# Exponential slots of two and two PSUM banks, and 576 instead of 456 score tiles on VectorE, in a kernel that mixes softmax attention with linear attention

## The chip, the cores and the metric

The kernel runs on one core of a Trainium2 chip, as one launch. The metric is device time in microseconds (us), the median of three runs. The engines of the core work side by side, each through its own list of instructions in a fixed order, and wait for each other by semaphores: TensorE (PE, with its weight loads as PEld) multiplies matrices into PSUM, ScalarE (ACT) computes exponentials, VectorE (DVE) and GpSimd (POOL) do elementwise work, and SP issues DMAs. PSUM has eight banks of 512 fp32 columns.

## What is computed

Two attention layers read the same input, and a gate per row mixes them. Layer B is softmax attention over 2048 rows with 32 heads of 16 columns; layer A is linear attention with a learned feature map.

```
def _B_ref(x, wqkv, wo):
    ...
    scores = jnp.einsum("bhqd,bhkd->bhqk", q, k) * (Dh ** -0.5)
    p = _softmax(scores, axis=-1)
    o = jnp.einsum("bhqk,bhkd->bhqd", p, v)
    return (lambda x, *d: x.transpose(*d))(o, 0, 2, 1, 3).reshape(B, S, D) @ wo
x = A_x
g = _sigmoid((x * gate_w).sum(-1, keepdims=True))
a = _A_ref(x, A_wqkv, A_w_phi, A_wo)
b = _B_ref(x, B_wqkv, B_wo)
return g * a + (1 - g) * b
```

In `_A_ref`, queries and keys go through a 16 by 16 matrix per head and two softmaxes over 16 features, and the sums over all rows are small matrices per head. Nearly all of the time goes into the scores of layer B: 32 heads of 2048 by 2048.

## The kernel before

**Tiles and blocks.** The scores are computed transposed, 128 keys by 512 queries at a time; such a score tile fills one PSUM bank. A block is four heads (one per 32-row strip of TensorE, `i`) with 512 queries; each of its heads has 16 tiles, so a block has 64 tiles, and there are 32 blocks, 2048 tiles. A score matmul (`qk_mm`, L782) uses 32 of the 128 rows, so that up to four of different heads run at once. A product matmul (`pv_mm`, L883) multiplies the exponentials with the values, 32 output columns per head, so that again four heads run at once; all products of a block add up in the one bank psO. A column of ones in the values gives the softmax's denominator.

**Two ways to an exponential.** Most tiles go through ScalarE. They are packed into slots (`slots`, filled by `next_tile`): an even slot has three tiles in the banks S0 to S2 of psS, an odd one has two in S3 and S4. `add_qk` (L786) writes a slot's scores, `add_exp` (L859, instruction at L862) takes them all in one instruction into the ring `Ebuf`, and `add_pv` (L903) multiplies the tiles of `PV_SETS` slots. Slot j+2 uses the banks of slot j. The other tiles go to VectorE, `DN[b]` of them in block b. `add_group` (L827) takes four at a time: for each, a matmul "dq" writes a score tile into a shared bank, and VectorE turns it into 16-bit integers whose bits, read as bf16, approximate the exponential (L840). Then two passes over the whole group (L853) add the constants STEPS, which gives two more such approximations. All three are multiplied with the values, three product matmuls ("terms") per tile instead of one.

**Shared banks.** psM and S5 (list `MISC`) are shared by the dq tiles and by every projection (`fill`, L591), such as keys, queries and values of layer B, the features of layer A (whose exponentials, L1105, run on ScalarE) and the output. psO is copied out at the end of a block (`add_norm`, L967), and only then may the next block's products begin.

**The order of the work.** It isn't written by hand. `Plan.add` notes for each operation an engine, an assumed duration, a priority and what it depends on. `Plan.layout` (L149) plays the program through with these durations and fixes each engine's order and each shared bank; `Plan.emit` writes the instructions and waits. In it, a dq tile may ride along with a round of scores if its strip is free and a bank is (`RIDE_TOL`); a scores operation has precedence when an exponential is due to end (`QK_TOL`, for even and odd slots); zero matmuls (`zero_mm`, L873) fill TensorE where its recent activity is low; and the VectorE passes of L853 and the products on GpSimd are kept apart (`lock`). A list of start points (`gates` and the constants ending in _AT and _PACE) ties projections to the exponential after which they may begin. Intermediate buffers are rings: four or so for the first result of a group and two or three for each of the other two (`rings`).

Of the kernel before, what the change touches and what calls it, by code (L numbers as in the profile page):

```python
# [27 lines left out]
STEPS = (35, 83)  # L28
ESCALE = math.log(2.0) / 2.0 ** 7

DN = (0, 10, 14, 16, 14, 16, 14, 16, 14, 16, 14, 16, 14, 16, 14, 16, 14, 16, 14, 16, 14, 16, 14, 16, 14, 16, 14, 16, 14, 16, 14, 12)
G_EARLY = 13
W_AT = 18.0
D_FIRST = 12
RIDE = 0.02
WINDOW = 3.41
ROWS = (0.0, 0.42, 0.65, 1.0, 1.15)
# [2 lines left out]
PE_CLASS = {"qk": 0, "dq": 0, "pv": 1, "term": 1, "zero": 1}  # L40
T_PRIO = 40.0
WARM = 4
DQ_PRIO, DQ_K = 0.0, 1.0
KG_AT, KG_PACE, QG_AT, QG_PACE = 40.0, 13.0, 270.0, 14.0
R1_AT, R1_PACE, R2_AT, R2_PACE, R3_AT, R3_PACE = 25.0, 14.0, 180.0, 14.0, 330.0, 25.0
TR_LAT, TR_ISSUE = 3.0, 0.4
OP_AT = 620.0
O_AT, O_PACE = 500.0, 10.0
PV_SETS = 3
RIDE_TOL = 0.22  # L50
DMA_PAD, T2_PAD = 1.0, 1.5
QK_TOL = (0.2, 0.65)
TURN_PAD = 4.0
G_DEEP = 6
K_AT, K_PACE, Q_AT, Q_PACE = 45.0, 13.0, 275.0, 13.5
PN = (1, 2, 1, 2, 1, 2, 1, 2, 1, 2, 1, 2, 1, 2, 1, 2, 1, 2, 1, 2, 1, 2, 1, 2, 1, 2, 1, 2, 1, 2, 1, 2)
D_AHEAD = 22.0
CONT = -60.0
EPAIRS = 5
ERING = 2 * EPAIRS  # L60
LAT, BANK_LAT = 0.12, 0.12
DVE_SCALE = 1.0
# [339 lines left out]
def _build(ctx, nc, A_x, A_wqkv, A_w_phi, A_wo, B_wqkv, B_wo, gate_w, out):  # L402
# [6 lines left out]
    def sem(name):  # L409
        return ctx.enter_context(nc.semaphore(name))  # L410

    xT = sb([128, KT, S], name="xT")
    WAT = sb([128, 8, D], name="WAT")
    Wp = sb([128, KT, 2 * D], name="Wp")
# [9 lines left out]
    vAf = sb([128, NT * 8 * 65], name="vA")  # L424
    vA = vAf[:].rearrange("p (a b c) -> p a b c", a=NT, b=8)
    phiK = sb([128, 8, 1024], name="phiK")
    Ebuf = sb([128, EPAIRS, 2560], name="E")
    Tx = sb([128, 2, 2048], name="Tx")
    EA = sb([128, 2, 1024], name="EA")
    half = sb([128, 64, 8], F32, name="half")  # L430
# [34 lines left out]
    bS = [Bank(f"S{i}", psS[:, 512 * i:512 * (i + 1)]) for i in range(6)]  # L465
    bO = Bank("O", psO[:])
    bM = Bank("M", psM[:])
    for b in range(3):
        bS[b].free = False
    FIRST = [bM, bO, bS[3], bS[4], bS[5]]  # L470
    EARLY = [bM, bO, bS[5]]
    MISC = [bM, bS[5]]

    P = Plan()

# [249 lines left out]

    while True:
        j = len(slots)
        act = [t for t in (next_tile() for _ in range(3 - j % 2)) if t is not None]
        if not act:
            break  # L730
        slots.append(act)
# [53 lines left out]

    def add_qk(j):  # L786
        ts = slots[j]
        base = 3 * (j % 2)
        reads = []
        for b, i, kt in ts:  # L790
            for k in (kkey(b // 8, kt), ("q", b // 2 % 4, b % 2)):
                if k not in reads:
                    reads.append(k)

        def fn(e):
            ins = None
            for m, t in enumerate(ts):
                ins = qk_mm(e, t, psS[:, 512 * (base + m):512 * (base + m + 1)])
            return ins
        op = P.add("pe", 0.25, -100, fn, reads=reads, writes=[("S", j % 2)], name=f"qk{j}")  # L800
        op.full = 0.21
        op.kind, op.heads = "qk", [t[1] for t in ts]
        if j < 2:
            op.margin = 0.1
        if j == 1:
            op.take = [bS[3], bS[4]]
        if j == 35:
            op.deps += xe
        return op

# [11 lines left out]

    def d_prio(d):
        b = d["t"][0]
        return first_slot[b] + d["k"] * 20.0 / DN[b] - D_AHEAD

    def add_group(g):  # L827
        t, s, m = (bufs[g[k]][0] for k in "tsm")
# [29 lines left out]

    def add_exp(j):  # L859
        n = len(slots[j])  # L860
        base = 3 * (j % 2)
        op = P.add("act", 0.051 + 0.4267 * n, 0.0, lambda e: e.activation(  # L862
            Ebuf[:, j // 2 % EPAIRS, 1536 * (j % 2):1536 * (j % 2) + 512 * n], psS[:, 512 * base:512 * (base + n)], ACTF.Exp, scale=ESCALE),
            reads=[("S", j % 2)], writes=[("E", j % ERING)], name=f"exp{j}")
        op.kind, op.extra = "exp", j % 2
        exp_ops[j] = op
        return op
# [35 lines left out]
    def add_pv(js):  # L903
        parts = {}
        for j in js:
            for m, t in enumerate(slots[j]):
                parts.setdefault(t[0], []).append((j, m, t))
        for b, jmts in parts.items():
            work, reads, seen = [], ["v1", "v2", "zero"], [0] * 4
            last = last_act[b] in [t for _, _, t in jmts]  # L910
            for j, m, t in jmts:
                start = (b, t[1]) not in pv_started
                pv_started.add((b, t[1]))
                o = 1536 * (j % 2) + 512 * m
                work.append((seen[t[1]], t, Ebuf[:, j // 2 % EPAIRS, o:o + 512], start))
                seen[t[1]] += 1
                for k in (("E", j % ERING), ("v", t[0] // 8, t[2] // 4)):
                    if k not in reads:
                        reads.append(k)
            rounds = max(seen)  # L920
            work.sort(key=lambda x: x[0])
            heads = [t[1] for n, t, _, _ in work if n == rounds - 1]
            cols = tuple(sum(x[0] == n for x in work) for n in range(rounds))
            work = [x[1:] for x in work]
            mts = [(m, t) for _, m, t in jmts]
            j = js[-1]

            opened_all = all((b, i) in pv_started for i in range(4))
            old = b in full_start

            def fn(e, work=work, last=last, j=j, b=b, old=old):
                ins = None
                for _ in range(zero_ops[j, b].extra):
                    zero_mm(e)
                for n, (t, rhs, start) in enumerate(work):
                    ins = pv_mm(e, t, rhs, start, last and n >= len(work) - 4)
                return ins
            first = any(t[1] == 0 and t[2] == 0 for _, t in mts)
            op = P.add("pe", 0.25 + 0.215 * (rounds - 1), -50, fn, reads=reads,
                       writes=["psO"] if first else (),  # L940
                       after=pv_last[-1:] + (block_pvd.get(b, []) if last else []), name=f"pv{j}")
            op.full = 0.215 * rounds
            op.kind, op.heads, op.cols = "pv", heads, cols
            op.room, op.alive = 2 if old else 0, opened_all and not last
            zero_ops[j, b] = op
            pv_last.append(op)
            if b not in full_start and all((b, i) in pv_started for i in range(4)):
                full_start[b] = op
                block_pvd[b] = []
                mine = [d for d in dtiles if d["t"][0] == b]  # L950
                for d in mine:
                    make_groups(d["g"]["n"] + 1)
                    assert made[0] > d["g"]["n"]
                    block_pvd[b] += add_pvd(d, op)
                if mine:
                    make_groups(mine[-1]["g"]["n"] + G_DEEP)
            if js[0] == 0:
                op.take = [bO]
            if first:
                op.margin = 1.0  # L960
            if last:
                add_norm(b, op)
# [82 lines left out]
    def out_last(i):  # L1045
# [9 lines left out]
                  writes=[("fin", tile % 4)], after=va_ops, name=f"Oe{tile}")  # L1055
        else:
            end = lambda e, ap: e.matmul(ap, lhsT=oT[:, 3, 3, 128 * i:128 * (i + 1)], rhs=WoB[:, 3, :], start=True, stop=True)
            f, mm = fill(-200 + i - 1.5, [end], [("oT", 3, 3), "WoB"], banks=bS[:5], name=f"O{tile}")
            drain(f, mm, "dve", 0.72, 0, lambda e, ap: e.scalar_tensor_tensor(
                fin[:, tile % 4, :], ap, omg[:, tile:tile + 1], osum[:, i - 2, :], ALU.mult, ALU.add),  # L1060
                  reads=["omg", ("part", i)], writes=[("fin", tile % 4)], after=va_ops, name=f"Oe{tile}")
# [167 lines left out]
        v_fill(0, c, 6.4 * c - 4.0, EARLY)  # L1229
    gates = {}  # L1230
    for qc in range(1, QC):
        gates[f"Q0.{qc}"] = 20 * qc
        q_fill(0, qc, 20.0 * qc)
    for c in range(QC):
        gates[f"K1.{c}"], gates[f"V1.{c}"] = int(R1_AT + R1_PACE * c), int(R1_AT + R1_PACE * (c + 4))
        k_fill(1, c, R1_AT + R1_PACE * c + 5)
        v_fill(1, c, R1_AT + R1_PACE * (c + 4) + 5)
        both = [v_pair(c, hf, R2_AT + R2_PACE * (c + 4 + hf / 2) + 5) for hf in range(2)]
        for hf in range(2):
            gates[f"V2.{c}.{hf}"] = int(R2_AT + R2_PACE * (c + 4 + hf / 2))  # L1240
        P.join_writes(both, ("v", 2, c))
        P.join_writes(both, ("v", 3, c))

    def k_row(r):
        at, pace = (R2_AT, R2_PACE) if r == 2 else (R3_AT, R3_PACE)
        for c in range(QC):
            gates[f"K{r}.{c}"] = int(at + pace * c)
            k_fill(r, c, at + pace * c + 5)

    gate()  # L1250
# [38 lines left out]
            k_row(k_next)  # L1289
            k_next += 1  # L1290
    for j in (NS - 2, NS - 1):
        exp_ops[j].rel = [bS[3 * (j % 2) + m] for m in range(3 - j % 2)]
    for op in P.ops:
        if op.name.startswith("Tq0."):
            op.deps = op.deps + wp_ops
# [7 lines left out]
    for op in P.ops:  # L1303
        if op.name.endswith(".0") and op.name[:-2] in gates:
            op.deps = op.deps + [exp_ops[gates[op.name[:-2]]]]
        for head, at, pace in (("P1.", KG_AT, KG_PACE), ("VA", KG_AT, KG_PACE), ("P0.", QG_AT, QG_PACE)):
            part = op.name[len(head):].split(".")
            if op.name.startswith(head) and len(part) == 2 and part[1] == "0" and part[0].isdigit():
                op.deps = op.deps + [exp_ops[min(NS - 40, int(at + pace * int(part[0])))]]

    P.idle, P.misc = zero_mm, MISC
    P.add("sp", 0.1, 1e6, lambda e: None, reads=[("out", i) for i in range(NT)], name="end")
# [36 lines left out]
```

## Time and profile before

| | |
|---|---|
| median of 3 runs | 777.43 us (777.22 to 778.01) |
| profiled execution, first to last instruction | 774.6 us |
| its mean granted TensorE clock | 0.991 |
| exponentials of 3 banks, of 2 banks | 318, 319 |
| conversions on VectorE (L840) | 456 |
| DMA | 30.72 MB, mean 40 GB/s |

The time of the profiled execution as a whole is not listed; its span lies 2.8 us below the median of the runs.

The page's second part cuts the span into 40 slices of 19.4 us, each digit the busy share in tenths:

```profile
PE   8999989998999999989999999998999998999999
...
DVE  3667877777778888567898897987887778787842
ACT  6999999999999999999999999999999999999996
...
PEclk9999999999999999998999999999999999999999
```

ScalarE is at 9 from the second slice to the last but one. VectorE is mostly at 7 or 8, with little to do in the first slice and the last two. TensorE's digits say less, because a matmul's row also holds the time in which it drains while the next one is already running. The trace gives the clock stretch by stretch: it is full except for three stretches at half speed, which begin about 345, 584 and 676 us from the start and last 6.8, 3.4 and 3.4 us.

Where a row is shown as "x318 | 518.2, 1629", 318 instructions were busy for 518.2 us and lasted 1629 ns each on average; rows of one engine can overlap at their ends, so the distance from start to start is what counts.

### The profile page before, as it was taken

The page shows a single profiled execution, that of the slowest core. Times are in us where ns is not written, and L with a number is a line of the kernel's source. Part 1 is how long each engine was busy: PE and PEld are TensorE (multiplying, and loading weights), DVE is VectorE, ACT ScalarE, POOL GpSimd, SP SyncE. Part 2 cuts the span into 40 slices and gives each one's busy share as a digit, 9 for nine tenths or more (in the row PEclk, how much of TensorE's full clock was granted, in tenths as well). Part 3 has the DMA queues.
Part 4 walks back from the last instruction along what each step waited for, and adds up shares of the span by engine and source line. Part 5 has one row for each costly group of instructions (what it writes and reads, how often), then busy time and mean ns, then how long its engine had stood idle before and what let it go on. Part 6 is the DMA issues. An engine that isn't in the chain of part 4 may idle for free.

```text
span 774.6 us, 17058 instructions
## 1 busy us (share of the span) xinstructions
PE 718.3 (93%) x7135; PEld 223.1 (29%) x7194; DVE 585.0 (76%) x1023; ACT 757.2 (98%) x708; POOL 137.0 (18%) x141
## 2 busy tenths in 40 slices
PE   8999989998999999989999999998999998999999
PEld 4332222332322222332322222222232222222222
DVE  3667877777778888567898897987887778787842
ACT  6999999999999999999999999999999999999996
POOL 6001032112322131200313121231311200000000
PEclk9999999999999999998999999999999999999999
DMA  6600000000000100201002221322311221020101
GB/s 128 146 9 16 20 14 21 10 23 9 10 17 9 24 8 8 72 8 23 23 27 60 55 71 44 82 68 51 83 53 38 73 53 37 22 64 3 46 13 48
DMA packets 67933, 30.72 MB, mean 40 GB/s; under 512 B 53208, under 2 KB 62808, under 8 KB 67856
## 3 DMA queue, kind: packets, MB, share of 16 engines
q1 hardware_dynamic: 66368, 28.95, 14.9%
q8 instruction: 56, 0.92, 0.5%
q10 hardware_dynamic: 1104, 0.66, 0.3%
q0 software_dynamic: 384, 0.02, 0.1%
q14 instruction: 21, 0.17, 0.1%
HBM read 7.87 MB, written 8.88 MB: 22 GB/s over the span
## 4 chain that ended last, share of the span: by engine, by line
ACT 84%; PE 11%; DVE 4%; SPq 1%; DMA 1%; issue 1%
ACT E_t L862 80%; ACT EA_t L1105 3%; PE psS L782 3%; PE psO L883 3%; PE psM L591 1%; PE psS L591 1%; DVE Tx_t L840 1%; DVE WAT_t L840 1%; PE psO L873 1%; DMA xT_t<-in_A_x_dram 1%; SPq L486 0%; DVE vA_t L853 0%; PE psS L651 0%; DVE vA_t L840 0%; DVE Ty_t L853 0%
## 5 line engine op out<-in xcount | busy, mean ns | idle before, releaser
L862 ACT ACTIVATE E_t<-psS 128x1536 bf16<-128x1536 f32 x637 | 731.9, 1419 | 5.4 <-PE psS L782 3.7
L782 PE MATMUL psS<-qz_t,kTB_t 32*128 32x512 bf16 x1815 | 277.0, 387 | 41.9 <-ACT E_t L862 34.1
L782 PEld LDWEIGHTS psS<-qz_t,kTB_t 32*128 32x128 bf16 x1815 | 69.2, 91 | 277.8 <-ACT E_t L862 242.3
L883 PE MATMUL psO<-E_t,vaug_t 128*32 128x512 bf16 (+1 forms) x1592 | 141.1, 389 | 0.7 <-DVE vaug_t L647 0.5
L840 DVE TENSOR_SCALAR Tx_t<-psS 128x512 int16<-128x512 f32 x121 | 82.4, 681 | 27.2 <-PE psS L782 24.6
L840 DVE TENSOR_SCALAR Tx_t<-psM 128x512 int16<-128x512 f32 x127 | 86.8, 683 | 19.4 <-PE psM L782 17.7
L873 PE MATMUL psO<-xT_t,zero_t 128*32 128x512 bf16 x1076 | 93.8, 387 | 0.0
L1110 POOL TENSOR_TENSOR half_t<-EA_t 128x512 f32<-128x512 bf16 x32 | 37.0, 1155 | 314.0 <-ACT EA_t L1105 273.4
L782 PE MATMUL psM<-qz_t,kTB_t 32*128 32x512 bf16 x233 | 90.1, 387 | 0.7 <-DVE Tx_t L840 0.2
L883 PE MATMUL psO<-vA_t,vaug_t 128*32 128x512 bf16 (+1 forms) x430 | 58.7, 387 | 0.0
L883 PE MATMUL psO<-Ty_t,vaug_t 128*32 128x512 bf16 (+1 forms) x308 | 50.4, 390 | 0.0
L1118 POOL TENSOR_TENSOR phiQ_t<-EA_t,stat_t 128x512 bf16<-128x512 bf16 x32 | 34.2, 1070 | 72.2 <-DVE stat_t L1114 61.7
L983 POOL TENSOR_TENSOR oT_t<-Tf_t,Rb_t 128x512 bf16<-128x512 f32 x15 | 19.1, 1272 | 157.4 <-DVE Ty_t L853 91.1
L883 PEld LDWEIGHTS psO<-E_t,vaug_t 128*32 128x32 bf16 (+1 forms) x1592 | 29.0, 95 | 59.8 <-issue 57.1
L1118 POOL TENSOR_TENSOR phiK_t<-EA_t,stat_t 128x512 bf16<-128x512 bf16 x32 | 33.8, 1058 | 60.4 <-DVE stat_t L1114 31.3
L883 PE MATMUL psO<-Tx_t,vaug_t 128*32 128x512 bf16 (+1 forms) x248 | 38.5, 398 | 0.0
L873 PEld LDWEIGHTS psO<-xT_t,zero_t 128*32 128x32 bf16 x1076 | 23.3, 94 | 41.3 <-issue 36.2
L853 DVE TENSOR_SCALAR vA_t<-Tx_t 128x2048 int16<-128x2048 int16 x50 | 34.1, 686 | 0.1
L853 DVE TENSOR_SCALAR Ty_t<-Tx_t 128x2048 int16<-128x2048 int16 x42 | 29.8, 709 | 0.4
L840 DVE TENSOR_SCALAR WAT_t<-psM 128x512 int16<-128x512 f32 x37 | 25.2, 682 | 5.9 <-PE psM L782 3.8
L840 DVE TENSOR_SCALAR WAT_t<-psS 128x512 int16<-128x512 f32 x39 | 26.6, 682 | 2.2 <-PE psS L782 1.9
L782 PEld LDWEIGHTS psM<-qz_t,kTB_t 32*128 32x128 bf16 x233 | 21.1, 91 | 23.1 <-issue 6.7
(188 smaller groups left out, 768.1 us busy)
## 6 DMA issues: line engine op xcount, KB each, us to landing
dpq<-phiQ_t SPq DMA_DIRECT2D x16, 256.0 KB, 2.1
Rb_t<-lr SPq DMA_DIRECT2D x120, 32.0 KB, 1.8
dpo<-oA_t SPq DMA_DIRECT2D x16, 128.0 KB, 1.8
qz_t<-qz_t SPq DMA_DIRECT2D x120, 16.0 KB, 1.8
Tf_t<-Tf_t SPq DMA_DIRECT2D x60, 32.0 KB, 2.0
out_dram<-WvA_t SPq DMA_DIRECT2D x14, 128.0 KB, 1.7
WB_t<-in_B_wqkv_dram SPq DMA_DIRECT2D x3, 384.0 KB, 4.4
WvA_t<-in_A_wqkv_dram SPq DMA_DIRECT2D x1, 512.0 KB, 4.0
```

Source lines behind the costliest of these rows:

```text
L591: return [lambda e, ap, i=i: e.matmul(ap, lhsT=lhs[i], rhs=rhs[i], start=(i == 0), stop=(i == len(lhs) - 1)) for i in range(len(lhs))]
L782: return e.matmul(bank, lhsT=kT_B[32 * i:32 * i + 32, b // 8 % 2, 128 * kt:128 * (kt + 1)], rhs=qz[32 * i:32 * i + 32, b // 2 % 4, b % 2, ...
L840: ops.append(drain(f, mm, "dve", 0.70, d_prio(d), lambda e, ap, q=q: e.tensor_scalar(quarter(tb, q).bitcast(I16), ap, EXPB, 0.0, op0=ALU.a ...
L853: add(0.72 if size == 4 else 0.45, lambda e, dst=dst, step=step: e.tensor_single_scalar(dst, t, step, ALU.add), tk, [g[key]], "D2" if key ...
L862: op = P.add("act", 0.051 + 0.4267 * n, 0.0, lambda e: e.activation(Ebuf[:, j // 2 % EPAIRS, 1536 * (j % 2):1536 * (j % 2) + 512 * n], psS ...
L873: ins = e.matmul((psO if bank is None else bank)[32 * i:32 * i + 32, :], lhsT=zero[:], rhs=xT[:, 0, 0:NQ], start=bank is not None, stop=ba ...
L883: return e.matmul(psO[32 * i:32 * i + w, :], lhsT=vaug[:, kt, o:o + w], rhs=rhs, start=start, stop=stop, tile_position=(0, 32 * i), skip_g ...
L983: P.add("pool", 1.1, -40, lambda e: e.tensor_tensor(oT[:, r, qc, :], Tf[:, 0, :], Rb[:], ALU.mult), reads=[("Tf", 0), "Rb"], writes=[("oT" ...
L1105: ins = e.activation(EA[:, b, :].rearrange("p (g s c) -> p s g c", s=2, c=64)[:, sgn, :, :], ap.rearrange("p (g c) -> p g c", c=64), ACTF. ...
L1110: P.add("pool", 1.15, prio, lambda e: e.tensor_tensor(half[:], e3[:, :, 0:8], e3[:, :, 8:16], ALU.add), reads=[("EA", b)], writes=["half"] ...
L1118: parts.append(P.add("pool", 1.0, prio, lambda e, n=n: e.tensor_tensor(dst[:, 512 * n:512 * n + 512].rearrange("p (g f) -> p g f", f=DH), ...
```

## The change

- The slots have two banks each: S0 and S1 for even ones, S2 and S3 for odd ones (`SIZES`). The ring `Ebuf` has six pairs of 2 + 2 tiles instead of five of 3 + 2.
- S4 becomes a shared bank: `MISC` is psM, S4 and S5.
- `DN` rises from 14 and 16 tiles in most blocks to 18 and 20 (22 and 20 in blocks 29 and 30), 576 in all instead of 456. Blocks 0, 1 and 31 keep 0, 10 and 12.
- Products are taken for four slots at a time (`PV_SETS`), which is eight tiles.
- What counts in slots is scaled by `SC` = 1.25: the gates, and the due times of the VectorE tiles.
- Some constants of the order change: `QK_TOL`, `DQ_K`, `G_EARLY` (the block from which another set of buffers is used), `G_DEEP` (how many groups may be entered ahead), `D_FIRST`, and the _AT and _PACE values.

No operation is added or dropped otherwise.

```diff
-DN = (0, 10, 14, 16, 14, 16, 14, 16, 14, 16, 14, 16, 14, 16, 14, 16, 14, 16, 14, 16, 14, 16, 14, 16, 14, 16, 14, 16, 14, 16, 14, 12)
-G_EARLY = 13
+DN = (0, 10, 18, 20, 18, 20, 18, 20, 18, 20, 18, 20, 18, 20, 18, 20, 18, 20, 18, 20, 18, 20, 18, 20, 18, 20, 18, 20, 18, 22, 20, 12)
+G_EARLY = 14
+SIZES = (2, 2)
+SC = 1.25
-D_FIRST = 12
+D_FIRST = 14
-DQ_PRIO, DQ_K = 0.0, 1.0
-KG_AT, KG_PACE, QG_AT, QG_PACE = 40.0, 13.0, 270.0, 14.0
+DQ_PRIO, DQ_K = 0.027, 1.299
-R1_AT, R1_PACE, R2_AT, R2_PACE, R3_AT, R3_PACE = 25.0, 14.0, 180.0, 14.0, 330.0, 25.0
+KG_AT, KG_PACE, QG_AT, QG_PACE = 41.939, 13.0, 270.429, 11.441
+R1_AT, R1_PACE, R2_AT, R2_PACE, R3_AT, R3_PACE = 36.575, 14.388, 170.604, 16.017, 313.139, 23.051
-OP_AT = 620.0
-O_AT, O_PACE = 500.0, 10.0
-PV_SETS = 3
+OP_AT = 641.751
+O_AT, O_PACE = 627.355, 10.348
+PV_SETS = 4
-QK_TOL = (0.2, 0.65)
+QK_TOL = (0.25, 0.2)
-G_DEEP = 6
-K_AT, K_PACE, Q_AT, Q_PACE = 45.0, 13.0, 275.0, 13.5
+G_DEEP = 8
+K_AT, K_PACE, Q_AT, Q_PACE = 41.797, 12.153, 275.0, 10.409
-EPAIRS = 5
+EPAIRS = 6
...
-    Ebuf = sb([128, EPAIRS, 2560], name="E")
+    Ebuf = sb([128, EPAIRS, 512 * (SZ[0] + SZ[1])], name="E")
...
-    FIRST = [bM, bO, bS[3], bS[4], bS[5]]
-    EARLY = [bM, bO, bS[5]]
-    MISC = [bM, bS[5]]
+    lowS = SIZES[0] + SIZES[1]
+    FIRST = [bM, bO] + bS[SIZES[0]:]
+    EARLY = [bM, bO] + bS[lowS:]
+    MISC = [bM] + bS[lowS:]
...
-        act = [t for t in (next_tile() for _ in range(3 - j % 2)) if t is not None]
+        act = [t for t in (next_tile() for _ in range(SZ[j % 2])) if t is not None]
...
-        base = 3 * (j % 2)
+        base = SZ[0] * (j % 2)
...
-        return first_slot[b] + d["k"] * 20.0 / DN[b] - D_AHEAD
+        return first_slot[b] / SC + d["k"] * 20.0 / DN[b] - D_AHEAD
...
-        gates[f"Q0.{qc}"] = 20 * qc
+        gates[f"Q0.{qc}"] = int(SC * 20 * qc)
```

The other lines replace 3 and 1536, as the size of an even slot, in the same manner, and scale the other gates by SC.

More of the change, by code (lines that the diff above doesn't have):

```diff
@@ L410, in sem @@
         return ctx.enter_context(nc.semaphore(name))
+    SZ = SIZES
     xT = sb([128, KT, S], name="xT")
@@ L467, in _build @@
     bM = Bank("M", psM[:])
-    for b in range(3):
+    for b in range(SIZES[0]):
         bS[b].free = False
-    FIRST = [bM, bO, bS[3], bS[4], bS[5]]
-    EARLY = [bM, bO, bS[5]]
-    MISC = [bM, bS[5]]
+    lowS = SIZES[0] + SIZES[1]
+    FIRST = [bM, bO] + bS[SIZES[0]:]
+    EARLY = [bM, bO] + bS[lowS:]
+    MISC = [bM] + bS[lowS:]
     P = Plan()
@@ L805, in add_qk @@
         if j == 1:
-            op.take = [bS[3], bS[4]]
-        if j == 35:
+            op.take = [bS[m] for m in range(SIZES[0], lowS)]
+        if j == int(35 * SC):
             op.deps += xe
@@ L860, in add_exp @@
         n = len(slots[j])
-        base = 3 * (j % 2)
+        base = SZ[0] * (j % 2)
         op = P.add("act", 0.051 + 0.4267 * n, 0.0, lambda e: e.activation(
-            Ebuf[:, j // 2 % EPAIRS, 1536 * (j % 2):1536 * (j % 2) + 512 * n], psS[:, 512 * base:512 * (base + n)], ACTF.Exp, scale=ESCALE),
+            Ebuf[:, j // 2 % EPAIRS, 512 * SZ[0] * (j % 2):512 * SZ[0] * (j % 2) + 512 * n], psS[:, 512 * base:512 * (base + n)], ACTF.Exp, scale=ESCALE),
             reads=[("S", j % 2)], writes=[("E", j % ERING)], name=f"exp{j}")
@@ L913, in add_pv @@
                 pv_started.add((b, t[1]))
-                o = 1536 * (j % 2) + 512 * m
+                o = 512 * SZ[0] * (j % 2) + 512 * m
                 work.append((seen[t[1]], t, Ebuf[:, j // 2 % EPAIRS, o:o + 512], start))
@@ L1057, in out_last @@
             end = lambda e, ap: e.matmul(ap, lhsT=oT[:, 3, 3, 128 * i:128 * (i + 1)], rhs=WoB[:, 3, :], start=True, stop=True)
-            f, mm = fill(-200 + i - 1.5, [end], [("oT", 3, 3), "WoB"], banks=bS[:5], name=f"O{tile}")
+            f, mm = fill(-200 + i - 1.5, [end], [("oT", 3, 3), "WoB"], banks=bS[:lowS], name=f"O{tile}")
             drain(f, mm, "dve", 0.72, 0, lambda e, ap: e.scalar_tensor_tensor(
@@ L1231, in _build @@
     for qc in range(1, QC):
-        gates[f"Q0.{qc}"] = 20 * qc
+        gates[f"Q0.{qc}"] = int(SC * 20 * qc)
         q_fill(0, qc, 20.0 * qc)
     for c in range(QC):
-        gates[f"K1.{c}"], gates[f"V1.{c}"] = int(R1_AT + R1_PACE * c), int(R1_AT + R1_PACE * (c + 4))
+        gates[f"K1.{c}"], gates[f"V1.{c}"] = int(SC * (R1_AT + R1_PACE * c)), int(SC * (R1_AT + R1_PACE * (c + 4)))
         k_fill(1, c, R1_AT + R1_PACE * c + 5)
@@ L1239, in _build @@
         for hf in range(2):
-            gates[f"V2.{c}.{hf}"] = int(R2_AT + R2_PACE * (c + 4 + hf / 2))
+            gates[f"V2.{c}.{hf}"] = int(SC * (R2_AT + R2_PACE * (c + 4 + hf / 2)))
         P.join_writes(both, ("v", 2, c))
@@ L1246, in k_row @@
         for c in range(QC):
-            gates[f"K{r}.{c}"] = int(at + pace * c)
+            gates[f"K{r}.{c}"] = int(SC * (at + pace * c))
             k_fill(r, c, at + pace * c + 5)
@@ L1291, in _build @@
     for j in (NS - 2, NS - 1):
-        exp_ops[j].rel = [bS[3 * (j % 2) + m] for m in range(3 - j % 2)]
+        exp_ops[j].rel = [bS[SZ[0] * (j % 2) + m] for m in range(SZ[j % 2])]
     for op in P.ops:
@@ L1308, in _build @@
             if op.name.startswith(head) and len(part) == 2 and part[1] == "0" and part[0].isdigit():
-                op.deps = op.deps + [exp_ops[min(NS - 40, int(at + pace * int(part[0])))]]
+                op.deps = op.deps + [exp_ops[min(NS - 40, int(SC * (at + pace * int(part[0]))))]]
     P.idle, P.misc = zero_mm, MISC
```

## The prediction

> **What bounds the kernel now.** I read the page's busy table first, then the chain that ended last, then the waits, then the groups by shape, then single rows in order of time.
>
> ```profile
> PE 718.3 (93%) x7135; PEld 223.1 (29%) x7194; DVE 585.0 (76%) x1023; ACT 757.2 (98%) x708; POOL 137.0 (18%) x141
> ...
> ACT 84%; PE 11%; DVE 4%; SPq 1%; DMA 1%; issue 1%
> ```
>
> ScalarE (ACT) has work in 757.2 of 774.6 us, and 84% of the chain lies on it. The waits (total us, times, longest us) show that almost nothing holds it up:
>
> ```profile
> ACT E_t L862 <- PE psS L782: 3.7, 5, 1.7
> ```
>
> So the sum starts from ScalarE's own rows. The two shapes of its exponential:
>
> ```profile
> L862 ACT ACTIVATE E_t<-psS 128x1536 bf16<-128x1536 f32 x318 | 518.2, 1629 | 4.9 <-PE psS L782 3.3 <-PE psM L782 1.4
> L862 ACT ACTIVATE E_t<-psS 128x1024 bf16<-128x1024 f32 x319 | 385.8, 1210 | 0.5 <-PE psS L782 0.4
> ```
>
> The means of 1629 and 1210 ns overlap with the next row and must not be added up. From start to start, where the next one follows without delay, a three-bank exponential takes 1.337 us and a two-bank one 0.909 us; the chain shows the same as single pieces:
>
> ```profile
> 157.55 1.34 ACT E_t L862
> ...
> 480.60 0.92 ACT E_t L862
> ```
>
> The span is 774.6 us and the median of the runs 777.43; I carry the 2.8 us between them along unchanged.
>
> **1. ScalarE gains 46.1 us.** 318 x 3 + 319 x 2 = 1592 score tiles are on ScalarE now, and 2048 - 1592 = 456 on VectorE. Then it is 576, which leaves 1472 tiles in 736 exponentials of two banks. Now: 318 x 1.337 + 319 x 0.909 = 715.1 us. Then: 736 x 0.909 = 669.0. The other ScalarE work is untouched. Alone this gives 777.4 - 46.1 = 731.3 us.
>
> The shorter form costs a little: 0.909 for two banks is 0.4545 per tile, 1.337 for three is 0.446, and the difference between the two forms, 0.428 per bank, leaves 0.053 us fixed per instruction. 99 more instructions cost 5 us, already in the sum. The Trainium skill, "ScalarE: Activation LUTs", section "What ACT_TABLE_LOAD costs", speaks more strongly against the change: 186 ns + 0.833 ns per column, less about 93 ns of overlap back to back, an estimate of 1.373 and 0.946 us, by which the gain would be 42.1 us instead of 46.1. The rows of this trace have less fixed cost, and the sum uses them.
>
> **2. The refill of a slot: 0 to 8 us.** A slot is refilled with scores while the other slot's exponential runs. So far the three-bank slot had 0.909 us for it and the two-bank slot 1.337. After a two-bank exponential, the next one started more than 0.97 us later 38 times out of 319. Without the last (before the end) and three beside half-speed stretches of the clock, that is 34 times and 6.3 us over the normal step. Then every refill has only 0.909 us: 736/319 x 6.3 = 14.5, or 8 us more. The lower end is nothing, since only two heads instead of three must be finished. This delay is no addition if another engine is later anyway.
>
> **3. VectorE gets 108.7 us.** A tile there costs one conversion out of PSUM (L840), and a group of four costs two further passes (L853).
>
> ```profile
> L840 DVE TENSOR_SCALAR Tx_t<-psM 128x512 int16<-128x512 f32 x127 | 86.8, 683 | 19.4 <-PE psM L782 17.7 <-PE psS L782 1.0
> ```
>
> Two of these back to back, in the order in time (start, length, engine, line):
>
> ```profile
> 465.25 0.69 DVE L853 TENSOR_SCALAR vA_t<-WAT_t 128x2048 int16<-128x2048 int16 x1
> 465.86 0.68 DVE L840 TENSOR_SCALAR vA_t<-psM 128x512 int16<-128x512 f32 x1
> ```
>
> A row lasts 0.68 us, but the next starts 0.60 to 0.61 later. So 120 x 0.606 = 72.7 us. Counting the groups of four from the two lists DN: 106 now, 136 then; the 16 half groups stay. 30 x 2 x 0.60 = 36.0. Sum 108.7 us.
>
> Is there room? The lengths of all 1024 VectorE rows add up to 642 us; less 0.08 each, laid end to end, they need 560. Of these 10 lie before 30 us and 10 after 740, where the start and the last block leave VectorE little to do. Between lie 540 us in 710, and then 540 + 109 = 649. ScalarE's pace makes that stretch 710 - 46.1 x 710/756 = 666.7 us. So VectorE must be in use for 649/666.7 = 97% of it, without a pause. In the same measure (rows less 0.08) the best that it does now is 96% over 20 us, 88% over 40 us and 87% over 60 us, though nobody drives it harder now. This is the crux: **VectorE becomes the bound, or nearly**.
>
> What it really loses: pauses under 0.5 us ahead of its rows add up to 34 us between 30 and 740 us, over about 960 rows, 0.035 each. About 1140 rows then lose 40 us. I take these as unavoidable (a handover between engines each) and the 136 us of longer pauses as free, since they are largely times without a tile to do. 649 + 40 = 689 us, 22.3 more than ScalarE's 666.7. **731.3 + 22.3 = 753.6 us.** The 8 us of step 2 vanish under it.
>
> Bounds of the unknown: nothing lost (0 us, then steps 1 and 2 give 731 to 739), or the share that held over 40 us, 0.88 (649/0.88 = 737.5, 70.8 over ScalarE, 802 us). I take the value nearest to the rows of single pauses, a share of 0.94.
>
> **4. The freed bank.** Conversions and all projections share two banks now, psM and one of psS; the waits have VectorE standing ahead of L840 for scores (L782) 25.6 us on psS and 19.9 on psM for the buffers Tx alone. A third bank lets TensorE write the next tile while two are being read. The gain lies within the 0 to 40 us of step 3; by itself it moves nothing, since ScalarE is the bound today.
>
> **5. TensorE: 66 us more work, covered.** I grouped the matmuls that start together into rounds: 805 with scores, 832 with products, 308 zero rounds (L873, filling). A round after one of its kind starts 0.216 us later, after another kind 0.32. The zero rounds are 308 x 0.216 = 66 us; delays beyond these steps are 76 us. So real work is 775 - 66 - 76 = 633. Added: 99 more score rounds with a change of kind on each side, 99 x 0.426 = 42; of the 456 tiles for VectorE, 805 - 637 = 168 needed a round of their own, the rest rode in a ScalarE round; the same share of 120 is 44 x 0.216 = 9.5; products rise from 2960 (1592 + 3 x 456) to 3200, at 3.56 per round 67 rounds, 14.5. Sum 66, making 699 us in 754: 93%. Its cover is the zero rounds and delays, 142 us. If that is gone, TensorE is the end itself (rival 3).
>
> **6. What costs nothing.** No DMA is added, and nothing is put into SP's or GpSimd's queue; the gates' numbers of exponentials are multiplied by 1.25, while 736/637 is 1.155, so where their constant stays they come 8% later in the order; I price that at nothing, since the same projections follow and only their place among the tiles moves; if they bunch, VectorE pauses, and the price is inside the bounds of step 3. GpSimd is busy 18%. L853 and GpSimd disturb each other: 18 of the 213 full-length rows lay beside a GpSimd product and lasted 1.08 us instead of 0.68; 60 more rows at that share cost 60 x 18/213 x 0.4 = 2 us, inside the 40. The exponentials' ring holds 24 tiles instead of 25, 10.9 us of ScalarE work.
>
> **Rivals.**
> 1. *VectorE keeps up* (0.16). The third bank removes even the short pauses, and ScalarE sets the end: 731 to 739 us, with step 2 in force **739**. For it: stretches of 10 us now run without any pause. Against: 97% for 667 us.
> 2. *VectorE falls behind, slower* (0.23). Place: the last products of a block (L883 with start of L967, the copy of psO) need all of its VectorE tiles. A late group holds the product bank; the ring of 10.9 us fills; ScalarE waits at every block. Price: 649/s - 666.7. At s = 0.88 this is 70.8, **802 us**. It decides from 649/s - 666.7 = 46.1, s = **0.910**: below, the change loses. For it: no stretch of 40 us reaches this today. Against: ScalarE was the bound, so VectorE had no reason to.
> 3. *TensorE becomes the bound* (0.09). If the VectorE tiles no longer find room in the score rounds (the free bank must come up just then), all 576 take one: (576 - 212) x 0.216 = 79 us, 699 + 79 = 778, so about **780 us**. For: 93% is already little slack. Against: a round now has two free heads, not one or two.
>
> That exponentials do not all have two banks is excluded by the lists: 1472 is even, and blocks follow without a break.
>
> **The numbers.** Forecast (step 3, 740 to 775 us): 0.52. Rivals 0.16, 0.23, 0.09. About 0.2% (1.6 us) is what a measurement of this kernel can tell from no change. Of rival 3 I put 0.05 within it and 0.04 above. Faster 0.52 + 0.16 = 0.68, same 0.05, slower 0.27. The range goes from 735, between the floor and rival 1's time, to 800, at rival 2's price: about 0.07 is left out below and 0.12 above.
>
> **What would show it.** Right: 736 exponentials of 1024 columns, 0.909 us apart where nothing delays; VectorE busy near 690 us and over 90% of the span's middle; TensorE's zero rounds far below 308; ScalarE pauses totalling 20 to 30 us that end with scores or products, behind VectorE. Wrong: ScalarE still at 98% (rival 1); long VectorE pauses before L840 that end with L782 while ScalarE waits too (rivals 2 and 3); a clock at half speed for longer than now, which would lengthen every round.

## The result, and the profile after

The changed kernel takes **737.9 us** (median of 4 runs, 737.3 to 739.1) against 777.5 (777.2 to 778.0): a ratio of 0.950, 95% interval 0.948 to 0.952. It gains 39.6 us; 23.8 were forecast. The time is that of rival 1, "VectorE keeps up" (739 us), not that of the forecast (753.6). In four of the kernels tried below (e1, e4, e5_old_g14, e8) some executions took two to four per cent longer at a lower granted clock and are left out of the times, but the shares, pauses and waits of e1, e5_old_g14 and e8 are read from such an execution, with the clock at half speed for 51 to 58 us from 17 to 24 us on.

The busy table, the chain by engine, and the slices of the kernel after:

```profile
span 735.5 us, 16772 instructions
...
PE 702.2 (95%) x6851; PEld 212.1 (29%) x6906; DVE 670.1 (91%) x1203; ACT 713.0 (97%) x807; POOL 137.2 (19%) x141
...
PE   8999999999999999999999999999999999999999
...
DVE  3567999899999999998999999999999999899963
ACT  6999999999999999999999999999999999999994
...
PEclk9999999999999999999999999999999998999999
...
ACT 67%; PE 18%; DVE 12%; issue 1%; SPq 1%; DMA 1%
```

VectorE is at 9 nearly everywhere, ScalarE too. ScalarE's part of the chain falls from 84% to 67%; what it lost runs over TensorE and VectorE in short pieces. The groups and the waits ahead of exponentials and conversions (the lines' numbers lie 5 further down now: L867 is the exponential, L787 the scores, L845 the conversion, L858 the two passes, L888 the products):

```profile
L867 ACT ACTIVATE E_t<-psS 128x1024 bf16<-128x1024 f32 x736 | 685.8, 1158 | 6.3 <-PE psS L787 4.9
...
L845 DVE TENSOR_SCALAR Tx_t<-psS 128x512 int16<-128x512 f32 x193 | 127.1, 677 | 4.5 <-PE psM L787 2.1
```

```profile
ACT E_t L867 <- PE psS L787: 4.9, 6, 1.7
...
DVE Tx_t L845 <- PE psS L787: 3.6, 7, 1.5
...
DVE Tx_t L845 <- PE psM L787: 2.8, 3, 1.4
```

The same waits of VectorE before (total us, times, longest us):

```profile
DVE Tx_t L840 <- PE psS L782: 25.6, 30, 3.7
DVE Tx_t L840 <- PE psM L782: 19.9, 27, 1.8
```

So the waits ahead of the conversions into Tx fall from 25.6 and 19.9 us to 3.6 and 2.8, though VectorE converts 120 tiles more. The windows show two stretches in which nothing was left over on VectorE or ScalarE (columns: stretch, its length, then PE, PEld, DVE, ACT and POOL busy, and further on the clock):

```profile
150.00:200.00 50.00, 48.20 (x471) 14.79 (x468) 50.00 (x85) 49.94 (x60) 10.99 (x10) 1.00 0.07 13
...
400.00:450.00 50.00, 48.11 (x495) 13.65 (x497) 49.55 (x98) 50.00 (x60) 17.46 (x16) 1.00 0.25 62
```

VectorE 50.00 and ScalarE 49.94 us of 50: both run without a pause side by side.

**Where the time went.** The distances from exponential to exponential, without delays, now sum to 736 x 0.908 = 668.3 us instead of 715.1: 46.8 less. Delays in between grew from 10.8 to 14.0 us, and the wait behind the last exponential from 4.2 to 7.2. That leaves 46.8 - 3.2 - 3.0 = 40.6 us, of which the span shows 774.6 - 735.5 = 39.1; the first exponential starts 0.3 us later and the end behind the wait is 1.0 us longer.

### The profile page after: what moved, and what is told of

Same layout as the page of the kernel before. It is cut to its first block, busy times and chain, and to the rows that moved or that the text cites. A ratio compares the mean times of both kernels' runs of the same rounds, so it can differ in the third digit from the quotient of the medians.

```text
span 735.5 us, 16772 instructions
## 1 busy us (share of the span) xinstructions
PE 702.2 (95%) x6851; PEld 212.1 (29%) x6906; DVE 670.1 (91%) x1203; ACT 713.0 (97%) x807; POOL 137.2 (19%) x141
## 4 chain that ended last, share of the span: by engine, by line
ACT 67%; PE 18%; DVE 12%; issue 1%; SPq 1%; DMA 1%
ACT E_t L867 63%; PE psS L787 7%; PE psO L888 5%; ACT EA_t L1110 4%; PE psS L596 3%; DVE Tx_t L845 3%; DVE WAT_t L845 2%; DVE vA_t L858 2%; DVE vA_t L845 2%; PE psM L596 1%; DVE oA_t L1198 1%; DVE Ty_t L858 1%; DMA xT_t<-in_A_x_dram 1%; PE psO L878 1%; SPq L491 1%
## 5 line engine op out<-in xcount | busy, mean ns | idle before, releaser
L867 ACT ACTIVATE E_t<-psS 128x1024 bf16<-128x1024 f32 x736 | 685.8, 1158 | 6.3 <-PE psS L787 4.9
L787 PE MATMUL psS<-qz_t,kTB_t 32*128 32x512 bf16 x1856 | 299.9, 387 | 23.4 <-ACT E_t L867 16.9
L787 PEld LDWEIGHTS psS<-qz_t,kTB_t 32*128 32x128 bf16 x1856 | 75.5, 91 | 289.5 <-ACT E_t L867 265.3
L845 DVE TENSOR_SCALAR Tx_t<-psS 128x512 int16<-128x512 f32 x193 | 127.1, 677 | 4.5 <-PE psM L787 2.1
L888 PE MATMUL psO<-E_t,vaug_t 128*32 128x512 bf16 x1472 | 120.6, 387 | 0.5 <-issue 0.3
L787 PE MATMUL psM<-qz_t,kTB_t 32*128 32x512 bf16 x192 | 74.1, 386 | 0.0
L845 DVE TENSOR_SCALAR Tx_t<-psM 128x512 int16<-128x512 f32 x99 | 67.1, 678 | 2.5 <-PE psS L787 1.5
L888 PE MATMUL psO<-vA_t,vaug_t 128*32 128x512 bf16 (+1 forms) x534 | 57.9, 385 | 0.0
L888 PE MATMUL psO<-Ty_t,vaug_t 128*32 128x512 bf16 x390 | 45.9, 390 | 0.0
L878 PE MATMUL psO<-xT_t,zero_t 128*32 128x512 bf16 x492 | 43.3, 385 | 0.0
L858 DVE TENSOR_SCALAR vA_t<-Tx_t 128x2048 int16<-128x2048 int16 (+1 forms) x59 | 39.4, 679 | 3.2 <-PE psO L888 3.2
L1123 POOL TENSOR_TENSOR phiQ_t<-EA_t,stat_t 128x512 bf16<-128x512 bf16 x32 | 33.9, 1058 | 34.2 <-DVE stat_t L1119 16.6
L888 PE MATMUL psO<-Tx_t,vaug_t 128*32 128x512 bf16 x292 | 39.6, 385 | 0.0
L888 PEld LDWEIGHTS psO<-E_t,vaug_t 128*32 128x32 bf16 x1472 | 25.2, 95 | 47.5 <-issue 45.1
L845 DVE TENSOR_SCALAR vA_t<-psS 128x512 int16<-128x512 f32 x57 | 37.6, 679 | 1.2 <-PE psM L787 0.6
L845 DVE TENSOR_SCALAR WAT_t<-psS 128x512 int16<-128x512 f32 x57 | 37.6, 677 | 0.1
L858 DVE TENSOR_SCALAR Ty_t<-Tx_t 128x2048 int16<-128x2048 int16 (+1 forms) x53 | 35.2, 664 | 0.4 <-PE psO L888 0.4
L845 DVE TENSOR_SCALAR phiQ_t<-psS 128x512 int16<-128x512 f32 x40 | 26.5, 676 | 3.9 <-PE psM L787 2.6
L1110 ACT ACTIVATE EA_t<-psS 128x512 bf16<-128x512 f32 x48 | 29.3, 735 | 0.0
```

Of the source, the lines that this page charges most:

```text
L787: return e.matmul(bank, lhsT=kT_B[32 * i:32 * i + 32, b // 8 % 2, 128 * kt:128 * (kt + 1)], rhs=qz[32 * i:32 * i + 32, b // 2 % 4, b % 2, ...
L845: ops.append(drain(f, mm, "dve", 0.70, d_prio(d), lambda e, ap, q=q: e.tensor_scalar(quarter(tb, q).bitcast(I16), ap, EXPB, 0.0, op0=ALU.a ...
L858: add(0.72 if size == 4 else 0.45, lambda e, dst=dst, step=step: e.tensor_single_scalar(dst, t, step, ALU.add), tk, [g[key]], "D2" if key ...
L878: ins = e.matmul((psO if bank is None else bank)[32 * i:32 * i + 32, :], lhsT=zero[:], rhs=xT[:, 0, 0:NQ], start=bank is not None, stop=ba ...
L888: return e.matmul(psO[32 * i:32 * i + w, :], lhsT=vaug[:, kt, o:o + w], rhs=rhs, start=start, stop=stop, tile_position=(0, 32 * i), skip_g ...
L1110: ins = e.activation(EA[:, b, :].rearrange("p (g s c) -> p s g c", s=2, c=64)[:, sgn, :, :], ap.rearrange("p (g c) -> p g c", c=64), ACTF. ...
```

## The experiments

The theory after the result: ScalarE's tiles are the gain, and the freed bank is what lets VectorE take them without pauses. The rivals: VectorE could always have done it; or the bank gives a gain of its own; or the constants of the order do. For every run I measured VectorE's rows laid end to end (length less 0.08 us) as a share of the time from 30 us to 35 us before the end, and the pauses between them, split at 0.5 us.

| kernel | tiles on VectorE | shared banks | time, us | VectorE's share | pauses under 0.5 us, per row | longer pauses, us |
|---|---|---|---|---|---|---|
| before | 456 | 2 | 777.5 | 0.761 | 0.034 | 136 |
| after | 576 | 3 | 737.9 | 0.951 | 0.007 | 25 |
| e1 | 576 | 2 | 864.0 | 0.780 | 0.033 | 142 |
| e8 | 456 | 2 | 800.1 | 0.723 | 0.033 | 176 |
| e3 (slots 3+2) | 576 | 2 | 853.7 | 0.807 | 0.032 | 116 |
| e9 (slots 3+2) | 484 | 2 | 786.5 | 0.779 | 0.035 | 122 |
| e2 | 456 | 3 | 787.9 | 0.749 | 0.015 | 169 |
| e7 | 518 | 3 | 761.8 | 0.846 | 0.010 | 97 |
| e6 | 604 | 3 | 771.8 | 0.938 | 0.007 | 35 |
| e4 (old constants) | 576 | 3 | 776.3 | 0.920 | 0.008 | 47 |
| e5_g13 | 576 | 3 | 760.9 | 0.922 | 0.009 | 44 |
| e5_old_g14 | 576 | 3 | 751.6 | 0.912 | 0.008 | 49 |
| e10 | 576 | 3 | 744.3 | 0.943 | 0.008 | 29 |

The engines' orders are laid out anew in each of these kernels, with the constants that its row names, so a row also contains how well those constants suit it. Two pairs differ in the shared bank alone: the kernel after and e1, and e2 and e8.

**E1, the changed kernel with S4 left unused.**

```diff
-    MISC = [bM] + bS[lowS:]
+    MISC = [bM] + bS[lowS + 1:]
```

(and EARLY likewise.)

> The changed kernel with S4 left unused, so that VectorE's tiles and the projections share two banks (psM and S5) as before. Theory (the third bank is what lets VectorE run without pauses): its pauses ahead of conversions that end with scores come back, 30 us or more, VectorE's share of the stretch 30 to 705 us falls from 95% to 90% or less, and the time is 760 us or more. Rival (VectorE always could, it only had too few tiles): within 1% of the changed kernel, 735 to 745 us.

Measured: 864.0 us, 126 more than the changed kernel. The theory holds, and its bound was far too mild. The waits of ScalarE and VectorE in this kernel:

```profile
ACT E_t L867 <- PE psO L888: 99.9, 29, 9.4
```

```profile
DVE Tx_t L845 <- PE psS L787: 22.1, 29, 3.1
DVE Tx_t L845 <- PE psM L787: 17.8, 32, 1.5
DVE oT_t L845 <- PE psM L787: 16.2, 10, 8.5
```

VectorE stands ahead of conversions into Tx for nearly as long as before the change (39.9 us against 45.5). It is late with most blocks, the products cannot close the block, the ring of exponentials fills, and ScalarE waits 29 times, 99.9 us, for products. All of these 99.9 us lie later than 80 us. From 80 us on the pauses under 0.5 us are 0.034 per row in both e1 and e8, as in their rows of the table. This is the mechanism of rival 2, at the place that it named.

**E2, the changed kernel with the old list DN.**

```diff
-DN = (0, 10, 18, 20, 18, 20, ...
+DN = (0, 10, 14, 16, 14, 16, ...
```

> The changed kernel with the list DN of before: slots of 2+2 and three shared banks, but 456 tiles on VectorE. Theory (the whole gain is ScalarE's 120 tiles): 1592 tiles are 796 exponentials, 60 more than with 576, so 737.9 + 60 x 0.909 = 792 us, slower than before by the price of the shorter slot. Rival (the freed bank takes stalls away by itself): clearly below 780 us.

Measured: 787.9 us, ratio to before 1.014 (1.011 to 1.018). The theory's 792 is nearly met. Slots of two banks and the third shared bank, without more tiles on VectorE, make the kernel slower: the shorter slots cost more than the bank brings.

**E8, both: S4 unused and 456 tiles.** Edits of E1 and E2 together.

> Slots of 2+2, S4 unused so that two banks are shared, and the list DN of before (456 tiles on VectorE). Theory (the third bank only counts when VectorE must be full): within 1% of the same with three banks, 787.9 us, so 782 to 796 us. Rival (slots of two banks need the third shared bank in any case): 805 us or more.

Measured: 800.1 us (800.0 to 809.7), ratio to before 1.034 (1.027 to 1.042). The median lies between the two expectations: the third bank is worth some 12 us at 456 tiles, more than the 1% that the theory allowed, against 126 at 576.

**E3, the kernel before with the list DN of the change alone** (slots 3+2, two shared banks).

> The kernel before with the list DN of the change alone: slots of 3+2, two shared banks, 576 tiles on VectorE. ScalarE's exponentials would take 295 x 1.337 + 294 x 0.909 = 661.7 us instead of 715.1. Theory (two shared banks cannot feed VectorE): VectorE pauses and ScalarE waits for it at the end of each block, so at least half of the 53 us is lost, 750 us or more. Rival (the bank is not needed): 724 to 735 us, faster than the change.

Measured: 853.7 us, ratio 1.098 (1.095 to 1.102). ScalarE waits for products here too:

```profile
ACT E_t L862 <- PE psO L883: 94.3, 31, 18.4
```

The rival (724 to 735) is out: the tiles without the bank do great harm.

**E9, the kernel before with only 28 tiles more.**

```diff
-DN = (0, 10, 14, 16, 14, 16, ...
+DN = (0, 10, 14, 18, 14, 18, ...
```

> The kernel before, slots of 3+2 and two shared banks, with 28 tiles more on VectorE (484; every odd block 18 instead of 16). ScalarE has some 11 exponentials less, 28 x 0.446 = 12.5 us. Theory (with two shared banks VectorE's pauses come from the banks, and 456 is near what it can take): at most half of the gain arrives, 771 us or more. Rival (VectorE had room, and only much more than this is too much): 763 to 768 us.

Measured: 786.5 us, ratio 1.013 (1.009 to 1.016). Not even a small part of the shift pays with two shared banks and the constants as they were, though VectorE had been busy only 76% of the span before.

**E4, the changed kernel with the old start points, paces, priorities, QK_TOL, G_EARLY, G_DEEP and D_FIRST.**

> The changed kernel with the start points, paces and priorities of before (DQ_K, QK_TOL 0.2, G_EARLY, G_DEEP, D_FIRST, all _AT and _PACE). Theory (the gain is the tiles that moved; the constants are a small part): 738 to 752 us. Rival (the constants make VectorE's work even, and most of the gain hangs on them): 758 us or more, with VectorE's longer pauses above 50 us.

Measured: 776.3 us in the median, ratio 0.994 (0.990 to 0.998). The executions lie in two groups, four at 767.5 to 771.0 us and five at 776.3 to 778.3, so that 30 to 38 of the 39.6 us are gone. The time is the rival's: most of the gain hangs on the constants too. Its sign is missed by a little, as VectorE's longer pauses are 47 us and not above 50. In the profiled execution (767.5 us) VectorE has a hole from 310 to 345 us, and ScalarE waits shortly after it:

```profile
310.00:320.00 10.00, 9.85 (x74) 2.56 (x72) 4.57 (x8) 10.00 (x12) 3.11 (x3) 1.00 0.06 15
320.00:350.00 30.00, 29.30 (x307) 12.43 (x303) 19.31 (x32) 22.32 (x26) 4.42 (x4) 1.00 0.01 2
```

VectorE is busy 4.57 of 10 and 19.31 of 30 us, and then ScalarE 22.32 of 30.

**E5, G_EARLY by itself.** Groups from this block on use buffers in the memory of vA, which comes free only when the key features of layer A have been summed.

```diff
-G_EARLY = 14
+G_EARLY = 13
```

> The changed kernel with G_EARLY 13 instead of 14: groups from block 13 on take the buffers in the memory of vA, which come free only when the last key features of layer A are multiplied. Theory (that one constant makes the hole seen with the old constants, where VectorE was busy only 24 of 40 us between 310 and 350 and ScalarE waited 15 us): a hole of 10 us or more near 300 us, 748 to 756 us. Rival (the hole came from the start points and paces): 736 to 742 us.

Measured: 760.9 us, ratio to before 0.978 (0.975 to 0.981). The theory's hole is there, with a higher price than it gave (23 us against 10 to 18). VectorE's rows in order of time, with the idle time before each in brackets:

```profile
318.66 0.55 DVE L1119 RECIPROCAL stat_t<-stat_t 128x64 f32<-128x64 f32 x1
323.74 0.69 DVE L662 CAST vaug_t<-psM 128x512 bf16<-128x512 f32 x1 [4.52 <-PE psM L656]
327.40 0.42 DVE L1146 TENSOR_TENSOR kv_t<-kv_t,psS 128x260 f32<-128x260 f32 x1 [2.97 <-PE psS L1136]
332.04 0.42 DVE L1146 TENSOR_TENSOR kv_t<-kv_t,psS 128x260 f32<-128x260 f32 x1 [4.22 <-PE psS L1136]
332.38 0.69 DVE L858 TENSOR_SCALAR vA_t<-Tx_t 128x2048 int16<-128x2048 int16 x1
332.98 0.69 DVE L845 TENSOR_SCALAR vA_t<-psM 128x512 int16<-128x512 f32 x1
```

VectorE does three rows in 13 us; right behind the last sum (L1146) the passes into vA begin.

The counterpart, E4 with G_EARLY 14 and the other old constants:

> The changed kernel with the start points, paces and priorities of before, but G_EARLY 14. Theory (G_EARLY gives about half of what the old constants lost, the rest is many small pauses and a longer end): 750 to 762 us. Rival (all of it is G_EARLY): 738 to 745 us.

Measured: 751.6 us, ratio 0.968 (0.965 to 0.970), as the theory had it. So G_EARLY costs 23 us by itself and 16 to 25 beside the other old constants (E4's two groups), and all the others together 13.7.

**E10, G_EARLY 13 with earlier key features.**

```diff
-G_EARLY = 14
+G_EARLY = 13
-KG_AT, KG_PACE, QG_AT, QG_PACE = 41.939, 13.0, ...
+KG_AT, KG_PACE, QG_AT, QG_PACE = 38.75, 12.0, ...
-K_AT, K_PACE, Q_AT, Q_PACE = 41.797, 12.153, ...
+K_AT, K_PACE, Q_AT, Q_PACE = 38.6, 11.2, ...
```

> The changed kernel with G_EARLY 13, and layer A's key features 8% earlier in the order (KG_AT 38.75, KG_PACE 12.0, K_AT 38.6, K_PACE 11.2), which takes back what a scale of 1.25 adds over 736/637. Theory (with G_EARLY 13 VectorE stood until the last sum of the key features, L1146, had freed vA's memory): most of the 23 us between 13 and 14 come back, 738 to 748 us, and no pause of 5 us ahead of L1146 is left. Rival (block 13 in the late buffers costs by itself): 755 us or more.

Measured: 744.3 us, ratio 0.957 (0.955 to 0.959). 16.6 of the 23 us come back, and the 7.2 us that VectorE waited ahead of L1146 in E5, in two waits, are gone from its waits. (The expectation's sign, no pause of 5 us there, says little: the longest in E5 was 4.2.) So most of the hole came from the gates' lateness; 6.4 us stay unexplained.

**E6, 604 tiles** (20 in each block, 22 in block 29).

> The changed kernel with 604 tiles on VectorE (20 per block, 22 in block 29): VectorE has 28 x 0.606 us and up to 28 two-pass halves more, about 25 us, ScalarE 14 x 0.909 = 12.7 us less. Theory (at 576 VectorE is as full as it can be, so from here it sets the end): 748 to 765 us, with VectorE at 100% in the middle and ScalarE waiting. Rival (ScalarE is still the bound): 725 to 730 us.

Measured: 771.8 us, ratio 0.993 (0.991 to 0.995). The theory's side, and worse than its bound: 28 tiles more cost 34 us. The waits of ScalarE:

```profile
ACT E_t L867 <- PE psO L888: 37.1, 21, 6.3
```

At 576 tiles there is no such line in the answer. Products come late at 21 places, while there are 32 blocks. VectorE isn't at 100%, as was expected: its share is 0.938, below the 0.951 of 576 tiles. So the run shows blocks that end late, not a VectorE without a pause; the constants are those of 576 tiles, and no others were tried.

**E7, 518 tiles** (16 and 18, with 20 and 18 in blocks 29 and 30).

> The changed kernel with 518 tiles on VectorE (16 and 18 per block): ScalarE has 29 exponentials more, 26.4 us. Theory (at 576 ScalarE sets the end nearly everywhere, VectorE's fullness costs next to nothing): 737.9 + 26.4 = 764 us, within 4 us. Rival (VectorE's fullness already costs what ScalarE waits for, some 14 us): 748 to 756 us.

Measured: 761.8 us, ratio 0.980 (0.978 to 0.983). The theory's 764 within 2.2 us. Below 576 each tile moved is worth what ScalarE pays for it: (761.8 - 737.9) / 58 = 0.41 us, against 0.454 by its rows. So at 576 ScalarE still sets the end nearly everywhere, and VectorE's 95% costs some 2 us by this measure.

## Why the prediction was right in direction, and where it was wrong

1. **ScalarE's gain**: forecast 46.1 us, measured 46.8 in its own rows. E2 and E7 come near the same price per exponential (787.9 for 792, 761.8 for 764): 0.83 and 0.82 us of the 0.909.
2. **Refill**: forecast 6.3 to 14.5 us of delays away from the stretches of half clock, measured 8.6 (14.0 with the 5.4 beside such stretches). Small, as it said. (By the trace, the stretches before the change begin 349.5, 588.4 and 680.6 us from the first instruction, some 4 us later than the text on the profile before says.)
3. **The step that failed: "I take these as unavoidable (a handover between engines each)"**, 0.035 us per row, 40 us. Measured: 7.9 us over 1151 rows, 0.007 each. The table shows what they were. The five kernels with two shared banks have 0.032 to 0.035 per row, whether 456 or 576 tiles and whether slots of 3+2 or 2+2; all with three have 0.007 to 0.015. The pauses belonged to the banks: the two pairs that differ in the bank alone have 0.007 against 0.033 and 0.015 against 0.033. Step 4 itself had placed the bank's gain in the 0 to 40 us of step 3, and then the sum took its worst end by counting the pauses of the old arrangement. With 8 instead of 40, 649 + 8 = 657 us, below ScalarE's 666.7, and the sum becomes rival 1's. The rest of step 3 was sound: VectorE's rows, less 0.08 us each, grew from 558.9 to 662.9 us, 104.0 where 108.7 were forecast.
4. **"By itself it moves nothing"**: about right for the end (E2 is slower than before), though the bank is worth some 12 us between E8 and E2. What the step missed is how hard the bank is a condition: E3 loses 76 us without it (and E9 9 us, which may lie in the constants).
5. **TensorE**: forecast 948 score rounds and 899 rounds of products, counted 816 and 851. 736 rounds carry exponentials' scores, so only 80 rounds were dq's own; at one tile each, 496 of 576 rode along (86%, before 63%), as every such round has two free heads. Zero rounds went from 308 to 164. Rival 3's worry went the other way.
6. **Gates 8% later "at nothing"**: true only because G_EARLY was moved along. E5 and E10 show that the lateness costs 23 us where it meets the buffers in vA, and that bringing the features forward takes most of that away. The step said "VectorE pauses" as the way it would show; the place, a ring of buffers and not a bunching of projections, it did not name.
7. **Rival 2** was described rightly and lies one step further on: at 604 tiles, or at 576 with two banks, ScalarE waits for psO at the block ends. E9 suggests that the kernel before was already near that edge for two banks. Its point of decision, a share of 0.910, can't be read across kernels: E4's profiled execution has 0.920 and takes 767.5 us, E6 has 0.938 and takes 771.8.
8. **Luck and signs.** That the time comes within 1.1 us of rival 1's 739 is partly luck: the 8 us that rival 1 has for the refill are in truth 3.2 us of delays, 3.0 behind the last exponential and 1.3 at the two ends. Of the forecast's own signs, the zero rounds fell as it said; but VectorE was busy 670 us, not near 690, ScalarE waited 5.7 us for scores ahead of its exponentials, not 20 to 30 behind VectorE, and its 97% of the span are nearly the 98% that were to speak for rival 1.

**What stays open.** The kernels with two banks were not fitted to their banks as the changed one may be to its three; E4 puts a price of 30 to 38 us on constants alone. The losses of E1 and E3 (126 and 116 us over the changed kernel) are well above that, that of E9 (9 us over before) isn't: whether its loss comes from the banks or from the constants is not shown. No kernel was tried with two shared banks and constants fitted to it.

## What to carry to other kernels

Idle time of an engine is no room as long as its input buffers make the idle time: VectorE was 24% idle, and 28 more tiles, with nothing else changed, made the kernel 1.3% slower. Before charging pauses of today's trace to a changed kernel, ask which resource makes them and whether the change touches it. And when three engines end up full, the order counts as much as the amounts: one constant that decides when a set of buffers is used was worth 23 us.

## What the runs showed of the hardware

- VectorE can be kept without a gap for long: 50.00 us busy of 50, and over 60 us its rows, laid end to end, fill 0.999 of the time, over 100 us 0.995.
- The granted clock varies between executions of one program: E4 took 767.5 to 768.3 us in three at 0.989 and 776.3 to 778.3 in five at 0.974, on the same chip. What decides it is not shown.
- VectorE's passes beside GpSimd stay dearer: 28 of 272 full-length rows in the kernel after overlapped a GpSimd row and lasted 0.98 us on average instead of 0.68; by the same count it was 22 of 212 and 0.99 us before. The Trainium skill, "SBUF — State Buffer", section "Who interferes with whom", has VectorE in its two-port modes and GpSimd exclude each other for a whole instruction; the rows agree in kind, with 0.30 us more on average.
